# An attention kernel whose hand-written order of work gets a finer model of GpSimd, of the transfer queue and of a ring of buffers

## The chip, the cores and the metric

The kernel runs on one core of one Trainium2 chip. The core has five engines that run in parallel, each in the order of its own instruction list: TensorE (PE, matrix products), VectorE (DVE), ScalarE (ACT), GpSimd (POOL) and SyncE (SP, which only starts transfers). They work on an on-chip memory and on PSUM, the accumulators that PE writes. The metric is the time of one execution in microseconds (us), as the device counts it. The kernel before takes 2528.87 us, median of 3 runs (2528.14 to 2532.28).

## What is computed

Four residual layers on one sequence of S = 2048 rows of D = 512, with H = 32 heads of 16: layers A, B, A, B. A is softmax attention; B is linear attention with a learned feature map. Cut to what matters:

```python
def _A_ref(x, wqkv, wo):
    q, k, v = qkv[0], qkv[1], qkv[2]
    scores = jnp.einsum("bhqd,bhkd->bhqk", q, k) * (Dh ** -0.5)
    p = _softmax(scores, axis=-1)
    o = jnp.einsum("bhqk,bhkd->bhqd", p, v)
    return o.transpose(0, 2, 1, 3).reshape(B, S, D) @ wo
def _B_ref(x, wqkv, w_phi, wo):
    pq, pk = einsum("bhsd,hdf->bhsf", q, w_phi), einsum("bhsd,hdf->bhsf", k, w_phi)
    phi = concatenate([softmax(p), softmax(-p)])          # of q and of k
    o = phi_q (phi_k^T v) / (phi_q (phi_k^T 1) + 1e-6)
    return o.reshape(B, S, D) @ wo
x = x + _A_ref(_layernorm(x), ...); x = x + _B_ref(_layernorm(x), ...)   # twice
```

## The kernel before

Each attention layer has 32 **groups**: a group is a set of four heads (g, eight of them; two make an *octet*) and one block j of 512 queries. A group goes over 16 tiles of 128 keys, in two halves each, so a layer has 1024 **score tiles**. For a score tile PE does eight matmuls (`score_cols`, line L1171 of the profile; 0.217 us in the planner, `UNIT`), and ACT takes the exponential of 128x1024 scores into a buffer p (L1178). For two tiles together PE does a **value step** (`pvs`, L1221; `STEP`, 0.864 us), p against the values v, into an accumulator that lives for the group. Accumulators and all side work share two slots of PSUM, `double` and `pm`; `take()` gives out the one that came free first. About one tile in 40 has its exponential done by DVE instead (`power_task`, twelve instructions L1189 to L1209 on a PSUM slot; the text calls it a **power**).

At a group's end `norm_task` runs: two transposes on DVE empty the accumulator (`turned_sum`, L870), POOL adds the halves (L873), DVE forms the reciprocal (`rec`, L941 and L943) and the product `yn` (L948). Beside this PE has **side streams**: the projections of the next octet (`cols`, L702, in units of 0.217 us), whose results DVE and POOL turn into keys, queries and values (`kq_task`, `values_task`), the output projection of finished octets (`part`, `tail`), and in the first layer the scaling of weights (`prep_b`). Buffers with the tag yt form a ring of four: `turned_sum` and `kq_task` take them in turn, and a buffer of values is in use until SP has written it out in 16 transfers.

Two kinds of task take a **maximum over partitions** on POOL. `norms_task` (L923, nma) does it for each octet's norms, and from it okt and the shift row sh, which the keys of the octet need. `scale_task` (L345) does it for the weights of the next layer (sAo, sB, sBv and sBo, in the first layer). At the end of the program the smallest of all shifts (`lowest`, L1818) decides by such a maximum (`anybad`, L1822, then `flag`, L1824) whether a slower version has to be run. These four instructions are not in the hand-written order; the framework places them on their engines as early as their inputs are.

The order of all this on PE, DVE, ACT and POOL is written out when the kernel is built. `attention` steps a planner's clock `pe`. At each step it takes, in this order, a score tile when a score buffer is free, side work if it ends in time, or a value step if `pe + STEP <= max(due, free) + LATE` (due is when ACT would run dry). Tasks for DVE and POOL are generators which yield an engine, a cost in us and a rank; `Plan.advance` puts them on the two engines' clocks by rank and by when they are ready, and the instructions are emitted in that order. A cost that is too low thus lets an instruction be put ahead of one that would have been ready sooner; on the chip the engine then waits at it. `pairs(g)` starts the transfers that lay out the keys and queries of four heads, and `landed` is the time at which the planner takes them as done.

Of the kernel before, what the change touches and what calls it, by code (L numbers as in the profile page):

```python
# [9 lines left out]
F32 = mybir.dt.float32  # L10
# [7 lines left out]
P = 128  # L18
# [32 lines left out]
FAR = 1e9  # L51
# [6 lines left out]
LEAD = 8  # L58
REST = 0.0
VBUSY = 0.4  # L60
LATE = 0.15
SIDE = 0.0
# [9 lines left out]
def mha_hedgehog_stack(ctx, tc, x_in, a_wqkv, a_wo, b_wqkv, b_wphi, b_wo, out, shmin=SHMIN):  # L72
# [8 lines left out]
    np_ = pool("np", bufs=2)  # L81
# [253 lines left out]
    def scale_task(ms, name):  # L335

        m1 = ms[0]
        for i, m in enumerate(ms[1:]):
            yield "V", 0.17, 3
            t = cp.tile([P, 1], F32, name=f"{name}_m1{i}")  # L340
            nc.vector.tensor_tensor(t, m, m1, ALU.max)
            m1 = t
        yield "P", 1.0, 3
        mm = cp.tile([P, 1], F32, name=name + "_mm")
        nc.gpsimd.partition_all_reduce(mm, m1, P, bass_isa.ReduceOp.max)  # L345
# [448 lines left out]
    class LayerA:  # L794
# [37 lines left out]
        def take(self):  # L832
# [7 lines left out]
            return idx, [pair[:, h, :] for h in range(2)]  # L840

        def freed(self, idx):
            self.pfree[idx] = self.plan.end + 0.15
# [20 lines left out]
        def turned_sum(self, idx, ps, name, rank=0):  # L864

            ys = []
            for u in range(2):
                yield "V", 0.68, rank
                ys.append(np_.tile([P, 16, 32], F32, tag="yb" if u else "yt", name=name + str(u), bufs=2 if u else 4))
# [3 lines left out]
            nc.gpsimd.tensor_tensor(ys[0], ys[0], ys[1], ALU.add)  # L873
            return ys[0]

        def values_task(self, o, j, idx, ps):

            q = self.oct[o]
            yt = yield from self.turned_sum(idx, ps, "vyt")
            for a in range(4):  # L880
                for m in range(4):
                    dst = q["v"][32 * m:32 * m + 32, j * 528:(j + 1) * 528].rearrange("p (t x) -> p t x", x=132)
                    nc.sync.dma_start(dst[:, :, 33 * a + 1:33 * a + 33], yt[32 * a:32 * a + 32, m:16:4, :])  # L883

        def kq_task(self, o, j, ten, idx, ps, sqs):
# [3 lines left out]
            lo = stg[:, 0 if ten else 3, j * 512:(j + 1) * 512]  # L889
            cqk = con["qk"]  # L890
            yield "V", 0.75, 0
            tq = np_.tile([P, 512], F32, tag="yt", name="tq", bufs=4)
            nc.vector.tensor_scalar(tq, ps[0], cqk, None, op0=ALU.mult)
# [8 lines left out]
            yield "V", 0.7  # L902
            nc.vector.tensor_tensor(lo, tq, hi, ALU.subtract)

        def square_task(self, hi, sqs):
# [3 lines left out]
        def norms_task(self, o, i, idx, psn):  # L909
# [10 lines left out]
            nc.vector.tensor_reduce(m, q["nm"], AX.X, ALU.max)  # L920
            yield "P", 5.5
            mm = sp.tile([P, 1], F32, name="nma")
            nc.gpsimd.partition_all_reduce(mm, m, P, bass_isa.ReduceOp.max)  # L923
            yield "P", 1.5
            sh = self.shift_tile()
# [8 lines left out]
        def norm_task(self, G, idx, acc):  # L934

            g, j = self.groups[G]
            o, par = g // 2, g % 2
            yt = yield from self.turned_sum(idx, acc, "yt", -1)
            yield "V", 0.17, 0
# [5 lines left out]
            if par == 0:  # L945
                yn_hold[(o, j)] = np_.tile([P, 16, 32], F32, tag="yn", name="yn", bufs=5)
            yn = yn_hold[(o, j)]
            nc.vector.tensor_tensor(yn[:, :, par * 16:par * 16 + 16], yt[:, :, 1 - par:17 - par],  # L948
                                    rec.unsqueeze(2).to_broadcast([P, 16, 16]), ALU.mult)
            if par == 0:  # L950
                return
# [3 lines left out]
            yb = np_.tile([P, 512], F32, tag="yb", name="yb")  # L955
# [396 lines left out]
        def attention(self, extra, nxt):  # L1352
# [8 lines left out]
            plan = self.plan  # L1361
# [8 lines left out]
            def pairs(g):  # L1370
                self.alloc_pairs(g)
                self.load_pairs(g)
                self.landed[g] = plan.now + 16.0

# [8 lines left out]
            estart, slots, acc, pvdone = [], [0.0] * 6, {}, 0  # L1383
            pe = act = 0.0
            power, pxfree, rested = set(), 0.0, 0.0
            lost = 0.0
            with tc.manual_schedule(engines=COMPUTE):
                while pvq or any(s.gens for s in self.streams):
# [35 lines left out]
                    for turn in range(2):  # L1424
# [14 lines left out]
                        elif ready:  # L1439
                            G, kt = pvq[0]  # L1440
                            if (G in acc or min(self.pfree) <= pe) and pe + STEP <= max(due, free) + LATE:
# [16 lines left out]
                                break  # L1458
                        if turn == 0 and tiles and pxfree <= pe and rested <= pe and plan.clock["V"] <= pe + VBUSY:
                            n = NT * tiles[0][0] + tiles[0][1] + LEAD  # L1460
                            G, kt = n // NT, n % NT
                            if 0 < G < POWERS and self.groups[G][0] in self.kq and plan.now >= self.landed[self.groups[G][0]] and pvq[0][0] in acc and \
                               NT - pvq[0][1] >= 3 and min(self.pfree) <= pe and pe + UNIT <= max(due, free):
                                power.add((G, kt, 1))
                                pxfree, rested = FAR, pe + REST
                                idx, ps = self.take()
# [398 lines left out]
```

## Time and profile before

| | before |
|---|---|
| median of 3 runs | 2528.87 us |
| the profiled execution's own time | 2528.14 us |
| its span | 2526.1 us |
| granted clock of PE, mean | 0.987 |
| attention of layer 1 | 71 to 1027 us |
| layer B after it, with the next layer's start | 1027 to 1338 us |
| attention of layer 3 | 1338 to 2276 us |

A profile page has the busy time of each engine, the span in 40 slices, the chain of work that ended last, and the costliest groups of instructions. A group's row has line, engine, operation, output and inputs, count, then busy time, mean duration in ns, the idle time before these instructions and what ended it. A row of the timeline has start in us, duration in us, engine, line, operation and operands, the count merged into the row, and in brackets the idle time of that engine before it with what ended it ("issue" is idle time in which the engine waited for nothing that the trace shows).

### The profile page before, as it was taken

The numbers are of one execution on the slowest core, as the hardware profiler recorded it, in microseconds if no ns is written. First come the engines' busy times: TensorE is split into PE (matmuls) and PEld (weight loads), VectorE is DVE, ScalarE is ACT, GpSimd is POOL, SyncE is SP. The second block draws the span as 40 slices with busy tenths as digits, with TensorE's granted clock in tenths as the row PEclk, the third lists the DMA queues.
The fourth block names the chain that finished last, engine by engine and source line by source line (L and its number), as shares of the span: only waits on it lengthen the run. The fifth ranks groups of instructions, "written<-read, shape, count | busy, mean of one in ns | idle before, by whom it ended". The sixth has DMA issues, their size and how long they took to land.

```text
span 2526.1 us, 103429 instructions
## 1 busy us (share of the span) xinstructions
PE 2314.9 (92%) x46698; PEld 1090.1 (43%) x46698; DVE 1618.7 (64%) x2883; ACT 2129.0 (84%) x2378; POOL 535.2 (21%) x645
## 2 busy tenths in 40 slices
PE   6999998999999999889789999999899999998998
PEld 4444444444434444445344444444344344444543
DVE  8365636756666455889963666565575652468897
ACT  6999998999999999544438999999999999994553
POOL 3111111111111000366431112112111100005552
PEclk9999999999999999999889999999999999999999
DMA  5310530133036421100133004203300341110003
GB/s 194 66 27 8 87 64 18 53 46 57 3 92 160 140 81 57 35 18 17 68 95 62 17 7 61 34 3 51 64 3 11 72 135 63 60 69 26 9 18 110
DMA packets 114924, 142.85 MB, mean 57 GB/s; under 512 B 64184, under 2 KB 69928, under 8 KB 112168
## 3 DMA queue, kind: packets, MB, share of 16 engines
q1 hardware_dynamic: 113288, 133.38, 21.5%
q8 instruction: 367, 6.01, 1.0%
q0 software_dynamic: 1184, 2.77, 0.3%
q14 instruction: 85, 0.70, 0.1%
HBM read 62.16 MB, written 41.94 MB: 41 GB/s over the span
## 4 chain that ended last, share of the span: by engine, by line
ACT 51%; PE 20%; DVE 13%; issue 12%; POOL 3%; SPq 1%; DMA 1%; ACTq 0%; POOLq 0%; DVEq 0%
ACT p L1178 49%; PE s L1171 4%; PE double L1221 4%; PE pm L1221 2%; DVE su L1591 2%; PE pm L702 2%; PE po L685 1%; PE pbv L1521 1%; PE pk L1521 1%; POOL f L1600 1%; DVE f L1583 1%; SPq L883 1%; DVE f L1584 1%; DVE mx L1580 1%; PE pq L1521 1%
## 5 line engine op out<-in xcount | busy, mean ns | idle before, releaser
L1178 ACT ACTIVATE p<-s 128x1024 f32<-128x1024 f32 x2000 | 1846.5, 1068 | 47.6 <-PE s L1171 46.1
L1171 PE MATMUL s<-kq 49*32 49x512 f16 x15152 | 789.2, 382 | 96.1 <-ACT p L1178 79.7
L1171 PEld LDWEIGHTS <-kq 49*32 49x32 f16 x15872 | 387.7, 89 | 889.8 <-issue 814.4
L1221 PE MATMUL double<-p,v 64*32 64x512 f32 x8984 | 617.1, 592 | 2.4 <-DVE yt L870 1.1
L1221 PE MATMUL pm<-p,v 64*32 64x512 f32 x7016 | 479.6, 589 | 0.3 <-issue 0.3
L873 POOL TENSOR_TENSOR yt<-yt,yt 128x512 f32<-128x512 f32 x64 | 87.4, 1365 | 863.2 <-DVE yt L870 809.3
L1221 PEld LDWEIGHTS double<-p,v 64*32 64x32 f32 x8984 | 175.0, 106 | 32.1 <-PE pm L702 3.8
L1521 PEld LDWEIGHTS <-xnTa 128*128 128x128 f16 x1152 | 110.7, 98 | 155.2 <-DVE f L1584 28.5
L1600 POOL TENSOR_TENSOR f<-f,su 128x1024 f32<-128x1024 f32 x62 | 119.9, 1934 | 129.3 <-DVE su L1594 104.9
L1221 PEld LDWEIGHTS pm<-p,v 64*32 64x32 f32 x7016 | 136.0, 106 | 24.6 <-issue 2.2
L988 POOL TENSOR_TENSOR sq<-stg 128x512 bf16<-128x512 f16 x48 | 57.1, 1189 | 393.3 <-PE s L1171 293.4
L870 DVE STREAM_TRANSPOSE yt<-double 128x512 f32<-128x512 f32 x72 | 47.3, 696 | 131.5 <-PE double L1221 131.5
L1585 ACT ACTIVATE f<-f,c_pB 128x1024 f32<-128x1024 f32 x64 | 72.7, 1149 | 51.1 <-DVE f L1584 51.0
L1521 PE MATMUL pbv<-wbv,xnTa 128*128 128x512 f16 x384 | 91.6, 390 | 23.8 <-DVE f L1584 23.8
L1255 DVE SCALAR_TENSOR_TENSOR xt<-pm,c_oA,xt 128x512 f32<-128x512 f32 x52 | 38.9, 748 | 100.3 <-PE pm L702 87.5
L1255 DVE SCALAR_TENSOR_TENSOR xt<-double,c_oA,xt 128x512 f32<-128x512 f32 x60 | 44.8, 747 | 89.4 <-PE double L702 88.7
L1606 ACT ACTIVATE fk<-f 128x1024 f16<-128x1024 f32 x30 | 31.7, 1058 | 74.8 <-POOL f L1600 74.8
L702 PEld LDWEIGHTS <-wA 64*32 64x32 f16 x4608 | 75.9, 93 | 39.6 <-issue 1.4
L1521 PE MATMUL pq<-wbqk,xnTa 128*128 128x512 f16 x384 | 88.4, 379 | 0.0
L1521 PE MATMUL pk<-wbqk,xnTa 128*128 128x512 f16 x384 | 88.1, 379 | 0.0
L1591 DVE TENSOR_REDUCE su<-f 128x64 f32<-128x1024 f32 x64 | 77.5, 1211 | 9.5 <-ACT f L1585 8.9
L1203 DVE SCALAR_TENSOR_TENSOR px<-pz,px 128x512 f32<-128x512 f32 x96 | 74.0, 771 | 2.7
(320 smaller groups left out, 3087.9 us busy)
## 6 DMA issues: line engine op xcount, KB each, us to landing
kq<-stg SPq DMA_DIRECT2D x168, 128.0 KB
xd<-xt SPq DMA_DIRECT2D x40, 512.0 KB
xt<-xd SPq DMA_DIRECT2D x40, 512.0 KB
v<-vyt SPq DMA_DIRECT2D x384, 16.0 KB
oD<-osp SPq DMA_DIRECT2D x24, 256.0 KB
ob<-oD SPq DMA_DIRECT2D x8, 768.0 KB
xt<-in_A_x_dram SPq DMA_DIRECT2D x8, 512.0 KB
wbqk<-dBqk SPq DMA_DIRECT2D x2, 2048.0 KB
```

Of the source, the lines that this page charges most:

```text
L702: nc.tensor.matmul(ps[h][c, :], w[r, c], x[r], start=(n == 0), stop=(n == of - 1), skip_group_check=True)
L873: nc.gpsimd.tensor_tensor(ys[0], ys[0], ys[1], ALU.add)
L988: nc.gpsimd.tensor_tensor(sq, hi, hi, ALU.mult)
L1171: nc.tensor.matmul(banks2[u][32 * c:32 * c + 32, :], self.side(g, half, 64 * u, 0, kt * P + 32 * c, 32), self.side(g, half, 64 * u, 1, j * ...
L1178: nc.scalar.activation(pt, s, AF.Exp, scale=EXPS)
L1203: nc.vector.scalar_tensor_tensor(y, z, PB, y, op0=ALU.add, op1=ALU.mult)
L1221: nc.tensor.matmul(acc[h][32 * hh:32 * hh + 32, :], self.oct[o]["v"][r, x:x + 32], pt[r, hh % 2, :], start=(kt == 0), stop=(kt == NT - 1), ...
L1255: nc.vector.scalar_tensor_tensor(xt[:, u, :], ps[h], con["oA"], xt[:, u, :], op0=ALU.mult, op1=ALU.add)
L1521: nc.tensor.matmul(dst, xnT[:, a, c, t * P:(t + 1) * P], w(b, c), start=(i == 0 and c == 0), stop=(i == 2 and c == NC4 - 1))
L1585: nc.scalar.activation(f, f, AF.Exp, scale=con["pB"])
L1591: nc.vector.tensor_reduce(su, f[:, r, :], AX.X, ALU.add)
L1600: nc.gpsimd.tensor_tensor(f3, f3, self.part_sums(f3, slice(0, 64), factor), ALU.mult)
```

## The change

Costs in the planner: `scale_task` puts down 7.6 us instead of 1.0 for the maximum on POOL, `norms_task` 7.4 instead of 5.5 and then 2.1 instead of 1.5. The ring: a task that wants a yt buffer is held back in the plan until the planner's time of the fourth last buffer's release has come (`ring`, "until"); `ringed` takes the buffer, and the release times are set at the buffer's last use, for values by the time of the transfer queue, `self.sp`, plus 2.5. The queue: `self.sp` grows by 0.7 for each of the 16 transfers of values (`queued`) and by 17 for a set of `pairs`, whose `landed` is then `self.sp + 2` instead of the present time + 16. Value steps: `LATE` is 0.2 instead of 0.15. Powers: `REST`, which was 0, goes; in the first layer, before step 100, a power is only taken when no side work is due (`EAGER`). No computation is added or taken away, and no "until" becomes a wait of an engine: all of it moves instructions.

```diff
-REST = 0.0
+RING = 4
+EAGER = (100, 0)
-LATE = 0.15
+LATE = 0.2
@@ scale_task
-        yield "P", 1.0, 3
+        yield "P", 7.6, 3
@@ LayerA
+        def ring(self):
+            return "until", lambda: self.yts[-RING] <= self.plan.now
+        def ringed(self, name):
+            self.yts.append(FAR)
+            return len(self.yts) - 1, np_.tile([P, 16, 32], F32, tag="yt", name=name, bufs=RING)
+        def queued(self, n, cost):
+            self.sp = max(self.sp, self.plan.end) + n * cost
+            return self.sp
@@ turned_sum
+            if rank >= 0:
+                yield self.ring()
@@ values_task
-            yt = yield from self.turned_sum(idx, ps, "vyt")
+            slot, yt = yield from self.turned_sum(idx, ps, "vyt")
+            self.yts[slot] = self.queued(16, 0.7) + 2.5
@@ kq_task
+            yield self.ring()
             yield "V", 0.75, 0
-            tq = np_.tile([P, 512], F32, tag="yt", name="tq", bufs=4)
+            slot, tq = self.ringed("tq")
...
+            self.yts[slot] = self.plan.end + 0.1
@@ norms_task
-            yield "P", 5.5
+            yield "P", 7.4
...
-            yield "P", 1.5
+            yield "P", 2.1
@@ norm_task
+            self.yts[slot] = self.plan.end + 0.1
@@ attention, pairs
-                self.landed[g] = plan.now + 16.0
+                self.sp = max(self.sp, plan.now) + 17.0
+                self.landed[g] = self.sp + 2.0
@@ attention
-            power, pxfree, rested = set(), 0.0, 0.0
+            self.yts, self.sp = [0.0] * RING, 15.0
+            power, pxfree = set(), 0.0
...
-                        if turn == 0 and tiles and pxfree <= pe and rested <= pe and plan.clock["V"] <= pe + VBUSY:
+                        if turn == 0 and tiles and pxfree <= pe and (need is None or self.now >= EAGER[self.li]) and plan.clock["V"] <= pe + VBUSY:
```

What this does to the order is seen at three places. In the rows, the name left of the arrow is written and those right of it are read; numbers behind a name tell buffers apart. Line numbers of the changed kernel are higher by 1 to 28.

The first is on PE at the end of group 14 in the first attention. s is a score tile, a row that reads p is a value step, a row that reads xnT a projection. Before, from the last value step of the group on:

```order
L1221 MATMUL double<-p,v_1036 32x512 x8
L1171 LDWEIGHTS kq_0_6724
L1171 MATMUL s<-kq_0_6724 32x512
...
L702 MATMUL pm_11581<-xnT_0_154,wAv 32x512
...
L1171 MATMUL s<-kq_1_6725 32x512
...
L702 MATMUL pm_11582<-xnT_0_154,wAv 32x512
...
L1221 MATMUL double<-p,v_1036 32x512 x8
```

The first value step of the next group stands two score tiles later, in the same slot, behind two and then five units of projection. The same place in PE's order of the changed kernel:

```order
L1247 MATMUL pm_11018<-p,v_1036 32x512
L1197 LDWEIGHTS kq_0_6892
L1197 MATMUL s<-kq_0_6892 32x512
...
L703 MATMUL double<-xnT_1_155,wAv 32x512
...
L1197 MATMUL s<-kq_1_6893 32x512
...
L1197 MATMUL s<-kq_0_6892 32x512
...
L1247 MATMUL pm_11821<-p,v_1036 32x512
```

Now three score tiles lie between, the second and the third with two units of projection between them, and the value step follows the third. Of the 63 places in both layers where one group follows another, 25 have two tiles between and the same slot before, 23 three tiles and the same slot, and 15 change the slot; in the changed order these are 1, 49 and 12, and one has four tiles.

The second is on DVE in the second attention, around the norms' maximum of the last octet (nmx) and the end check that the framework places there. Before:

```order
L914 TENSOR_REDUCE nm<-pm_41862 128x1
L920 TENSOR_REDUCE nmx<-nm 128x1
L870 STREAM_TRANSPOSE yt_41967<-double 128x512
L870 STREAM_TRANSPOSE yt_41990<-double 128x512
L1818 TENSOR_REDUCE lowest<-okt 32x1
L1820 TENSOR_SCALAR bad<-lowest 32x1
L1189 TENSOR_SCALAR px<-double 128x512
L1192 SCALAR_TENSOR_TENSOR pw<-px,double 128x512
L941 TENSOR_SCALAR rec<-yt_41967 128x16
```

The flag stands ten rows below rec there. In the changed order of DVE the same place reads:

```order
L945 TENSOR_REDUCE nmx<-nm 128x1
L1235 SCALAR_TENSOR_TENSOR px<-pw,px 128x512
...
L1846 TENSOR_REDUCE lowest<-okt 32x1
L1848 TENSOR_SCALAR bad<-lowest 32x1
L1852 CAST flag<-anybad 32x1
L891 STREAM_TRANSPOSE yt_41910<-double 128x512
L891 STREAM_TRANSPOSE yt_41923<-double 128x512
L1215 TENSOR_SCALAR px<-double 128x512
L966 TENSOR_SCALAR rec<-yt_41910 128x16
```

The two transposes of the group's accumulator have moved from ahead of the check to behind its flag. The third place is on DVE at the end of the first attention: xnTa is the third block of the normalized rows, transposed, for layer B, and L1580 is layer B's first operation there. Before:

```order
L564 TENSOR_SCALAR xn<-xt,mv,ly 128x512 x2
L587 CAST xnTa_2_22782<-double 128x4x128
L592 TENSOR_TENSOR xnTa_2_22782<-double,xnTa_2_22782 128x4x128
L870 STREAM_TRANSPOSE yt_23649<-pm_23069 128x512
L870 STREAM_TRANSPOSE yt_23651<-pm_23070 128x512
L941 TENSOR_SCALAR rec<-yt_23649 128x16
L943 RECIPROCAL rec<-rec 128x16
L948 TENSOR_TENSOR yn<-yt_23649,rec 128x16x16
L1580 TENSOR_REDUCE mx<-pk 128x32
```

The transposes that empty the last accumulator come last there. In the changed order they come 24 rows ahead of the first row shown here, which stands among layer B's (L1608 to L1622):

```order
L982 STREAM_TRANSPOSE yb<-yn 128x512
L565 TENSOR_SCALAR xn<-xt,mv,ly 128x512
L985 CAST osp<-yb 128x512
L1612 TENSOR_TENSOR f<-mn,pq 128x32x16
L588 CAST xnTa_2_22881<-double 128x4x128
L1619 TENSOR_REDUCE su<-f 128x64
L593 TENSOR_TENSOR xnTa_2_22881<-double,xnTa_2_22881 128x4x128
```

The statistics, xn and the casts of the third block have moved behind the last transposes; a second cast and subtraction follow these.

More of the change, by code (lines that the diff above doesn't have):

```diff
@@ L868, in turned_sum @@
                 yield "V", 0.68, rank
-                ys.append(np_.tile([P, 16, 32], F32, tag="yb" if u else "yt", name=name + str(u), bufs=2 if u else 4))
+                if u == 0:
+                    slot, yt = self.ringed(name + "0")
+                    ys.append(yt)
+                else:
+                    ys.append(np_.tile([P, 16, 32], F32, tag="yb", name=name + "1", bufs=2))
                 nc.vector.transpose(ys[u].rearrange("p a b -> p (a b)"), ps[u])
@@ L873, in turned_sum @@
             nc.gpsimd.tensor_tensor(ys[0], ys[0], ys[1], ALU.add)
-            return ys[0]
+            return slot, ys[0]
         def values_task(self, o, j, idx, ps):
             q = self.oct[o]
-            yt = yield from self.turned_sum(idx, ps, "vyt")
+            slot, yt = yield from self.turned_sum(idx, ps, "vyt")
+            self.yts[slot] = self.queued(16, 0.7) + 2.5
             for a in range(4):
@@ L890, in kq_task @@
             cqk = con["qk"]
+            yield self.ring()
             yield "V", 0.75, 0
-            tq = np_.tile([P, 512], F32, tag="yt", name="tq", bufs=4)
+            slot, tq = self.ringed("tq")
+            tq = tq.rearrange("p a b -> p (a b)")
             nc.vector.tensor_scalar(tq, ps[0], cqk, None, op0=ALU.mult)
@@ L937, in norm_task @@
             o, par = g // 2, g % 2
-            yt = yield from self.turned_sum(idx, acc, "yt", -1)
+            slot, yt = yield from self.turned_sum(idx, acc, "yt", -1)
             yield "V", 0.17, 0
@@ L1464, in attention @@
                                 power.add((G, kt, 1))
-                                pxfree, rested = FAR, pe + REST
+                                pxfree = FAR
                                 idx, ps = self.take()
```

## The prediction

> **What bounds the kernel now.** I read the page first: the busy shares, then the costliest groups, then the chain that ended last.
>
> ```profile
> PE 2314.9 (92%) x46698; PEld 1090.1 (43%) x46698; DVE 1618.7 (64%) x2883; ACT 2129.0 (84%) x2378; POOL 535.2 (21%) x645
> ACT p L1178 49%; PE s L1171 4%; PE double L1221 4%; PE pm L1221 2%; DVE su L1591 2%; PE pm L702 2%; PE po L685 1%; PE pbv L1521 1%; PE pk L1521 1%; POOL f L1600 1%; DVE f L1583 1%; SPq L883 1%; DVE f L1584 1%; DVE mx L1580 1%; PE pq L1521 1%
> L1178 ACT ACTIVATE p<-s 128x1024 f32<-128x1024 f32 x2000 | 1846.5, 1068 | 47.6 <-PE s L1171 46.1
> ```
>
> PE has the most busy time, but the chain runs for 49% of the span through ACT's exponentials, line L1178. They stand in the two attention stages, so I asked for those two stretches alone (the columns are length, then busy time and count of PE, weight loads, DVE, ACT and POOL, granted clock, DMA share, GB/s).
>
> ```profile
> 71.00:1027.00 956.00, 894.73 (x21465) 410.46 (x21465) 557.69 (x1020) 925.11 (x1001) 114.03 (x111) 1.00 0.27 63
> 1338.00:2276.00 938.00, 881.86 (x21374) 400.56 (x21375) 528.48 (x937) 921.32 (x999) 113.98 (x104) 1.00 0.22 47
> ```
>
> There ACT does 1001 and 999 exponentials and is busy 97 and 98% of the time. Undisturbed they start every 0.915 us: in the row at 496.27 us further below, 31 of them take 28.52 us, so (28.52 - 1.07) / 30. At that pitch they need 916 and 914 us; 40 and 24 us are lost, and nearly all of it before an exponential that waits for PE's scores. So the attention stages can gain at most some 64 us, and a gain is one of scores that come in time. The change touches nothing outside the two stages but the order at their ends.
>
> **Part 1, stalls behind GpSimd and the ring: -12 us.** The longest losses in ACT's timeline were followed back through PE, DVE and POOL:
>
> ```profile
> 429.31 0.38 POOL L345 PARTITION_ALL_REDUCE sAo_mm<-sAo_m  x1 [5.85 <-issue]
> 437.12 1.25 POOL L873 TENSOR_TENSOR yt<-yt,yt 128x512 f32<-128x512 f32 x1 [7.43 <-issue]
> 438.40 0.17 DVE L941 TENSOR_SCALAR rec<-yt 128x16 f32<-128x16 f32 x1 [7.01 <-POOL yt L873]
> 439.30 0.55 PE L1171 MATMUL pm<-kq 49*32 49x512 f16 x7 [4.79 <-DVE tq L895]
> 440.38 1.02 ACT L1178 ACTIVATE p<-s 128x1024 f32<-128x1024 f32 x1 [4.84 <-PE s L1171]
> 442.52 23.94 ACT L1178 ACTIVATE p<-s 128x1024 f32<-128x1024 f32 x26 [1.11 <-PE s L1171]
> ...
> 528.84 1.27 POOL L873 TENSOR_TENSOR yt<-yt,yt 128x512 f32<-128x512 f32 x1 [6.91 <-issue]
> 534.58 1.02 ACT L1178 ACTIVATE p<-s 128x1024 f32<-128x1024 f32 x1 [3.27 <-PE s L1171]
> ...
> 852.21 1.25 POOL L873 TENSOR_TENSOR yt<-yt,yt 128x512 f32<-128x512 f32 x1 [7.10 <-issue]
> 855.36 3.02 ACT L1178 ACTIVATE p<-s 128x1024 f32<-128x1024 f32 x3 [1.56 <-PE s L1171]
> ...
> 136.03 0.75 DVE L893 TENSOR_SCALAR tq<-pm,c_qk 128x512 f32<-128x512 f32 x1 [2.55 <-DMA v<-vyt]
> 138.44 2.10 ACT L1178 ACTIVATE p<-s 128x1024 f32<-128x1024 f32 x2 [1.20 <-PE s L1171]
> ```
>
> A maximum over partitions holds POOL 5.85 us before its 0.38 us record and 6.9 to 7.4 us behind it, before the next sum. The planner had put down 1.0 us for that of a scale, so it placed rec, which needs the next sum, on DVE 7 us too soon; the operations behind rec in DVE's order stood, and with them the PSUM slot that PE wanted. The last pair is another cause: tq waits until the transfers of v have left its ring buffer. In the changed order on DVE, twelve operations of a power stand where rec stood behind sAo, and the same holds at the other maxima I followed, so I let these go: 4.84 + 1.11 + 3.27 + 1.56 + 1.20 = 12 us. What is late next there is nothing that I can find: the next sum on POOL now has no waiter. Bounds: 0 (below) and -14, with the small idle times that follow each.
>
> The wait itself is not added by the change: the new "until" for the ring holds back a task in the plan, not an engine. Only a projection's tq queues behind it in its own stream, and its slot of PSUM stays taken meanwhile.
>
> The page "GPSIMD Engine Reference" of the Trainium skill, section 2.1 on instruction dispatch, says that the first call of freshly loaded code pays about 6 us with no visible instruction. The rows agree (5.85 before, 6.9 to 7.4 behind), and by that rule each maximum holds POOL for two such loads, some 13 us, where the change puts down 7.4 or 7.6: a rule that speaks against it, and the reason for the second rival below.
>
> **Part 2, group ends: -21 us.** When the 16 value steps of a group are through, two transposes of DVE must empty the accumulator before the same PSUM slot serves the next group.
>
> ```profile
> 494.06 0.63 PE L702 MATMUL pm<-xnT,wA 64*32 64x512 f16 x16
> 494.86 1.09 PE L1221 MATMUL double<-p,v 64*32 64x512 f32 x16 [0.17 <-PE pm L702]
> 495.71 0.67 PE L1171 MATMUL s<-kq 49*32 49x512 f16 x16
> ...
> 496.27 28.52 ACT L1178 ACTIVATE p<-s 128x1024 f32<-128x1024 f32 x31 [0.64 <-PE s L1171]
> ...
> 2161.91 29.57 ACT L1178 ACTIVATE p<-s 128x1024 f32<-128x1024 f32 x32 [0.64 <-PE s L1171]
> ```
>
> Here the first value step of the next group follows two score tiles behind the last one, into the same slot, after projection matmuls, and the next scores come too late. I laid PE's order beside ACT's starts: 13 such ends in the first attention and 12 in the second, each with some 0.6 of idle ACT, as in the two rows, or up to 0.9; with the 0.15 by which the pitch is shorter than an exponential that is 0.7 to 1.1 each, 22 us in all. Ends with three tiles between cost 0.04, ends that change the slot 0 to 0.2. In the changed order one such end is left, 50 have three or four tiles between: -21 us, bounds -14 (if a third of the loss stays as value steps are put off) and -22.
>
> **Part 3, value steps closer together: +12 us.** With LATE at 0.2 and value steps put off at the ends, PE has to catch up.
>
> ```profile
> 654.15 0.41 PE L1171 MATMUL s<-kq 49*32 49x512 f16 x8 [0.34 <-ACT p L1178]
> 654.36 1.05 PE L1221 MATMUL double<-p,v 64*32 64x512 f32 x16
> 655.23 0.41 PE L1171 MATMUL s<-kq 49*32 49x512 f16 x8
> 656.30 0.41 PE L1171 MATMUL s<-kq 49*32 49x512 f16 x8
> 656.90 0.41 PE L1171 MATMUL s<-kq 49*32 49x512 f16 x8 [0.18 <-ACT p L1178]
> ```
>
> A tile with a value step takes PE 1.08 us (654.15 to 655.23), 0.165 over the pitch of 0.915. A single one is absorbed by the tile before; of two in a row the second shows. The order before has 62 such pairs, which cost 0.079 us each in ACT's starts, 4.9 us; the order after has 127, most of them in the places (right behind a group end) where those of before cost 0.13 to 0.16. 127 x 0.135 = 17, so +12. Bounds: 65 more at 0.079, +5; all at 0.165, +16. Another 52 tiles with three projection units ahead of a value step, at the 0.048 of the 13 there are now: +2.5. The powers fall from 48 to 47, one exponential more: +0.9.
>
> **Part 4, the check's flag in the second attention: +5.4 us.** The end check of the program (lowest, bad, anybad, flag) is moved up into the second attention by its own dependences. Before, POOL's sum, two powers and rec lay between bad and flag. After, flag is next behind bad on DVE, ahead of the two transposes that free the accumulator.
>
> ```profile
> 1946.89 0.41 PE L998 MATMUL pm<-sq,bones 64*32 64x512 bf16 x8
> 1951.48 0.38 POOL L923 PARTITION_ALL_REDUCE nma<-nmx  x1 [5.96 <-issue]
> 1961.45 0.68 POOL L930 TENSOR_SCALAR sh<-sh,neg 1x512 f16<-1x512 f16 x1
> 1968.19 0.38 POOL L1822 PARTITION_ALL_REDUCE anybad<-bad  x1 [6.06 <-issue]
> ...
> 1976.06 2.10 ACT L1178 ACTIVATE p<-s 128x1024 f32<-128x1024 f32 x2 [1.18 <-PE s L1171]
> ```
>
> From the norms' matmul to the end of nma 5.0 us; 7.0 until POOL's next operation (row at 528.84); 1.1 for okt, neg and sh; 6.06 + 0.38 + 0.1 to the flag; 1.3 for the transposes: 20.9. PE wants the slot for a power 17 tiles behind the norms, 15.6 us. It stalls 5.3 us.
>
> ```profile
> 434.00:439.00 5.00, 0.51 (x17) 0.03 (x2) 0.59 (x2) 1.54 (x2) 1.25 (x1) 1.00 0.02 5
> 439.00:441.00 2.00, 1.70 (x31) 0.92 (x38) 2.00 (x5) 0.62 (x1) 1.09 (x1) 0.61 0.00 0
> 441.00:443.00 2.00, 2.00 (x40) 0.99 (x32) 2.00 (x5) 0.89 (x2) 0.00 (x0) 0.54 0.00 0
> ```
>
> After the 4.79 us stall of PE the granted clock (the third column from the end) is 0.61 and 0.54 and ACT idles 1.11 more; I add 1.2 for that and take off the 1.18 lost there today: +5.4. Bounds: +3 (flag's wait begins earlier than I think) and +9. "TensorE: Matmul & The Clock Gate" of the Trainium skill, Part 1, puts the halving behind an idle window of about 3.4 us; the row agrees, and by that rule a stall of under 3.4 us here would cost nothing more, which makes +4.2.
>
> **Part 5, end of the first attention: +5 us.** The changed order puts transposed casts of the third block (xnTa) and its small statistics behind the last value step, among layer B's first operations.
>
> ```profile
> 1025.39 0.69 DVE L592 TENSOR_TENSOR xnTa<-double,xnTa 128x512 f16<-128x512 f32 x1
> 1029.80 0.45 DVE L941 TENSOR_SCALAR rec<-yt 128x16 f32<-128x16 f32 x1 [1.45 <-POOL yt L873]
> 1037.00:1050.00 13.00, 12.84 (x85) 6.55 (x84) 12.81 (x20) 6.25 (x8) 7.84 (x6) 1.00 0.00 1
> ```
>
> Today these end at 1026, under ACT's last exponentials. After, three pairs of a cast and a subtraction of 0.69 each, nine small ones of about 0.16 and two xn of 0.5 stand behind: 6.7, less the 1.45 in which DVE waited for POOL. The stage behind is full on DVE (12.81 of 13), so it comes through: +5, bounds +2 and +6. The second attention's end is unchanged.
>
> **The sum**, against the profiled execution of 2528.1 us (its span 2526.1 and 2.0 around it; the median of the runs is 2528.9, 0.03% above): -12 - 21 + 12 + 2.5 + 0.9 + 5.4 + 5 = -7.2, so **2521**.
>
> **Rivals.** *Catch-up dearer than the ends.* If pairs come so thick that the slack is not refilled between them, both steps of a pair show, 2 x 0.165 = 0.33; with half of them so, 0.25 each, 127 x 0.25 = 32, minus 4.9 is 27 instead of 12: 2536. From 0.24 a pair the change is slower than before by over 0.2%. For it: the largest single pairs of the trace cost 0.46 to 0.48. Against: none of the ordinary ones costs over 0.17. *POOL's load comes back.* The planned 7.4 or 7.6 holds one load and not two; if the four places of part 1 only move, their 12 us come back: 2533. Against: the sums behind have few waiters. *Flag and tail are hidden*, as their waits end before PE or layer B asks: without 5.4 and 5 it is 2511. *The ends do not gain*, since putting off the value step merely moves the same loss to the next tile (part 2 at -7): 2535; for it speaks only that PE is busy 94% of the stage.
>
> **Chances.** Forecast 0.50 (own range 2514 to 2528), flag and tail hidden 0.20, catch-up dearer 0.12, load comes back 0.13, ends do not gain 0.05. What a measurement of this kernel tells from no change is about 0.2%, 5 us: faster is under 2523.8, slower over 2533.9. Of the forecast 0.38 lies in faster, 0.12 in same; hidden is faster; of the load 0.03 faster, 0.08 same, 0.02 slower; of the dear pairs 0.02 same and 0.10 slower; of the ends 0.02 and 0.03. Faster 0.61, same 0.24, slower 0.15. The range leaves out 0.1 on either side: 2508 to 2534.
>
> **What would show it.** Right: no idle of over 3 us before an exponential of the first attention; ACT idle of 0.6 to 0.9 once per layer instead of 12 times; many idles of 0.1 to 0.2; one PE stall of about 5 us in the second attention with flag on DVE behind it, clock halved after it; xnTa casts beyond the last exponential. Wrong: a stall of PE behind any other maximum, or group ends that still idle ACT by 0.6.

## The result, and the profile after

The changed kernel takes 2510.65 us (median of 6 runs, 2508.70 to 2513.97) against 2529.31 us of the kernel before in the same runs. The ratio is 0.9928, with a 95% interval of 0.9915 to 0.9940: 18 us, or 0.7%, faster. The profiled execution took 2509.21 us, its span is 2507.3. The forecast was 2521 us, its range 2508 to 2534.

The first view is again the page: the chain that ended last, and the group of the exponentials (now line L1204; scores are L1197, value steps L1247).

```profile
ACT p L1204 56%; PE double L1247 2%; PE s L1197 2%; DVE su L1619 2%; PE pbv L1549 1%; PE po L686 1%; PE pk L1549 1%; PE pq L1549 1%; DVE f L1611 1%; PE pm L703 1%; POOL f L1628 1%; DVE f L1612 1%; DVE mx L1608 1%; DVE st L492 1%; DVE su L1620 1%
L1204 ACT ACTIVATE p<-s 128x1024 f32<-128x1024 f32 x2001 | 1852.0, 1064 | 21.7 <-PE s L1197 19.1
```

The chain runs through the exponentials for 56% of the span instead of 49%, and the idle time that waits for PE's scores is 19.1 us instead of 46.1. ACT is bound by the same work as before, with fewer gaps. The windows of the two attention stages (length, then busy time and count of PE, weight loads, DVE, ACT and POOL) say the same by stage:

```profile
71.00:1008.00 937.00, 886.25 (x21422) 407.05 (x21414) 513.58 (x949) 929.04 (x1004) 113.04 (x111) 1.00 0.27 63
1324.00:2256.00 932.00, 874.86 (x21334) 399.09 (x21327) 541.35 (x964) 920.62 (x997) 110.86 (x104) 0.99 0.22 47
```

From the first start of an exponential of a stage to the last, in ACT's timeline, the profiled executions divide like this. "Late" is what the order of DVE has behind the last transposes of that attention of the output sums, statistics, xn and casts of its blocks, in number times duration; 1.9 us of it, the first statistics of the last block, stand there in every order. The time of each exponential beyond the pitch of 0.914 us, added up by size, stands below (exponentials that start sooner than the pitch are left out).

| us | before | changed |
|---|---|---|
| first attention (exponentials) | 953.9 (1001) | 937.0 (1004) |
| layer B and the next layer's start | 313.8 | 315.8 |
| second attention | 935.8 (999) | 932.2 (997) |
| last layer B | 251.6 | 251.7 |
| late at the first, at the second end | 1.9, 1.9 | 8.5, 3.3 |
| losses of 0.6 and more (places) | 44.6 (39) | 14.5 (10) |
| losses of 0.2 to 0.6 | 7.0 | 5.7 |
| losses under 0.2 | 17.3 | 29.0 |

Three views answer to the parts of the prediction. The first is POOL's timeline around the maximum of sAo, and ACT's over the same stretch, with two group ends in it.

```profile
409.61 0.50 POOL L346 PARTITION_ALL_REDUCE sAo_mm<-sAo_m  x1 [5.81 <-DVE sAo_m L342]
424.46 1.18 POOL L1014 TENSOR_TENSOR sq<-stg 128x512 bf16<-128x512 f16 x1 [14.36 <-DVE stg L922]
...
404.01 66.69 ACT L1204 ACTIVATE p<-s 128x1024 f32<-128x1024 f32 x72
```

POOL still stands idle for 5.81 us ahead of the maximum. But its next work waits for DVE anyway and comes 14 us later, so nobody waits for it, and 72 exponentials run without a gap over a stretch in which the kernel before lost 4.84 and 1.11 us to this stall and 0.65 at a group end. The second view is PE's timeline behind a group end:

```profile
477.16 0.41 PE L1197 MATMUL s<-kq 49*32 49x512 f16 x8
477.38 1.06 PE L1247 MATMUL double<-p,v 64*32 64x512 f32 x16
478.24 0.41 PE L1197 MATMUL s<-kq 49*32 49x512 f16 x8
478.46 0.61 PE L1247 MATMUL double<-p,v 64*32 64x512 f32 x4
...
479.32 0.41 PE L1197 MATMUL s<-kq 49*32 49x512 f16 x8
```

Two value steps stand in two tiles in a row; the scores come 1.08 us apart twice, and ACT loses 0.166 at the second. This is the catch-up: 127 such pairs, 21.7 us in ACT's starts, 0.171 each (before 62 pairs and 4.9 us). The third view is the check's flag in the second attention, on DVE, on PE and on ACT, with the clock of PE (third column from the end of the windows):

```profile
1927.52 0.14 DVE L1848 TENSOR_SCALAR bad<-lowest 32x1 f32<-32x1 f32 x1
1934.81 0.14 DVE L1852 CAST flag<-anybad 32x1 int32<-32x1 f32 x1 [7.16 <-POOL anybad L1850]
1934.88 1.29 DVE L891 STREAM_TRANSPOSE yt<-double 128x512 f32<-128x512 f32 x2
1943.30 0.17 DVE L966 TENSOR_SCALAR rec<-yt 128x16 f32<-128x16 f32 x1 [5.68 <-POOL yt L894]
...
1936.23 0.63 PE L1197 MATMUL double<-kq 49*32 49x512 f16 x8 [4.89 <-DVE yt L891]
...
1937.41 1.02 ACT L1204 ACTIVATE p<-s 128x1024 f32<-128x1024 f32 x1 [4.86 <-PE s L1197]
1939.54 15.69 ACT L1204 ACTIVATE p<-s 128x1024 f32<-128x1024 f32 x17 [1.11 <-PE s L1197]
1956.58 9.27 ACT L1204 ACTIVATE p<-s 128x1024 f32<-128x1024 f32 x10 [1.35 <-PE s L1197]
...
1936.00:1938.00 2.00, 1.77 (x32) 0.69 (x39) 0.87 (x2) 0.59 (x1) 0.00 (x0) 0.50 0.00 0
1938.00:1940.00 2.00, 2.00 (x40) 0.70 (x32) 0.00 (x0) 0.89 (x2) 0.00 (x0) 0.50 0.00 0
```

DVE waits 7.16 us for the check's maximum with the two transposes behind it, PE 4.89 us for the accumulator they empty. The clock is at 0.50 for the 4 us that follow, which costs 1.11 more. After that rec waits 5.68 us for POOL's next sum, and a power behind rec in DVE's order comes 1.35 us late.

### The profile page after: what moved, and what is told of

It is laid out like the page before. It is cut to its first block, busy times and chain, and to the rows that moved or that the text cites. A ratio compares the mean times of both kernels' runs of the same rounds, so it can differ in the third digit from the quotient of the medians.

```text
span 2507.3 us, 103429 instructions
## 1 busy us (share of the span) xinstructions
PE 2305.4 (92%) x46698; PEld 1086.9 (43%) x46698; DVE 1596.5 (64%) x2867; ACT 2134.8 (85%) x2379; POOL 531.2 (21%) x645
## 4 chain that ended last, share of the span: by engine, by line
ACT 58%; PE 14%; issue 13%; DVE 12%; POOL 2%; DMA 0%; POOLq 0%; ACTq 0%; DVEq 0%
ACT p L1204 56%; PE double L1247 2%; PE s L1197 2%; DVE su L1619 2%; PE pbv L1549 1%; PE po L686 1%; PE pk L1549 1%; PE pq L1549 1%; DVE f L1611 1%; PE pm L703 1%; POOL f L1628 1%; DVE f L1612 1%; DVE mx L1608 1%; DVE st L492 1%; DVE su L1620 1%
## 5 line engine op out<-in xcount | busy, mean ns | idle before, releaser
L1204 ACT ACTIVATE p<-s 128x1024 f32<-128x1024 f32 x2001 | 1852.0, 1064 | 21.7 <-PE s L1197 19.1
L1197 PE MATMUL s<-kq 49*32 49x512 f16 x15136 | 789.3, 381 | 99.1 <-ACT p L1204 86.1
L1197 PEld LDWEIGHTS <-kq 49*32 49x32 f16 x15872 | 386.0, 89 | 880.6 <-issue 798.5
L1247 PE MATMUL double<-p,v 64*32 64x512 f32 x9064 | 612.8, 591 | 0.0
L1247 PE MATMUL pm<-p,v 64*32 64x512 f32 x6944 | 476.6, 590 | 0.0
L1247 PEld LDWEIGHTS double<-p,v 64*32 64x32 f32 x9064 | 174.0, 106 | 30.9 <-issue 6.4
L1281 DVE SCALAR_TENSOR_TENSOR xt<-pm,c_oA,xt 128x512 f32<-128x512 f32 x102 | 76.2, 747 | 155.0 <-PE pm L703 151.1
L1247 PEld LDWEIGHTS pm<-p,v 64*32 64x32 f32 x6944 | 135.2, 106 | 22.2 <-issue 3.3
L891 DVE STREAM_TRANSPOSE yt<-pm 128x512 f32<-128x512 f32 x56 | 36.8, 696 | 89.9 <-PE pm L1247 89.6
L917 DVE TENSOR_SCALAR tq<-double,c_qk 128x512 f32<-128x512 f32 x28 | 21.0, 749 | 107.0 <-PE double L703 103.7
```

The source lines that it names most:

```text
L1197: nc.tensor.matmul(banks2[u][32 * c:32 * c + 32, :], self.side(g, half, 64 * u, 0, kt * P + 32 * c, 32), self.side(g, half, 64 * u, 1, j * ...
L1204: nc.scalar.activation(pt, s, AF.Exp, scale=EXPS)
L1247: nc.tensor.matmul(acc[h][32 * hh:32 * hh + 32, :], self.oct[o]["v"][r, x:x + 32], pt[r, hh % 2, :], start=(kt == 0), stop=(kt == NT - 1), ...
L1281: nc.vector.scalar_tensor_tensor(xt[:, u, :], ps[h], con["oA"], xt[:, u, :], op0=ALU.mult, op1=ALU.add)
```

## The experiments

Theory A: the new costs of the maxima keep work that depends on POOL away from them, and that removes the stalls. Theory B: LATE alone moves the group ends, and the stalls go because the ends no longer meet the maxima. The first four kernels tell them apart; from their results came theory C, on the ends of the attentions.

**LATE alone, and all but LATE.** The edit of the first is to the kernel before, that of the second to the changed one:

```diff
-LATE = 0.15
+LATE = 0.2
```

> The kernel before with LATE 0.2 and nothing else. Its order has no group end left with two tiles between in the same slot (25 before), 132 pairs of value steps in consecutive tiles (62 before), four exponentials fewer, and the flag right behind bad on DVE as in the changed kernel. Both theories: group ends -22.2, pairs (at 0.171 us each, the mean in the changed kernel's trace) +17.7, exponentials -3.7, flag +5: together -3.2 us. Theory A, the new costs on POOL remove the stalls behind the maxima: the 12 us of stalls stay, so about 2526 us. Theory B, the stalls go because LATE moves the group ends away from the maxima, whatever the costs say: about 2514 us.

```diff
-LATE = 0.2
+LATE = 0.15
```

> The changed kernel with LATE back at 0.15: only costs, transfer queue, ring and EAGER. 23 group ends with two tiles between in the same slot, 57 pairs, five exponentials more than before (+4.6 us), the flag right behind bad (+5). Theory A (costs remove the stalls): -12 us on top, about 2526 us. Theory B (LATE moves the group ends): the stalls stay or change places, about 2537 us.

LATE alone: 2538.21 us, ratio 1.0032 (1.0020 to 1.0044), slower than before; its profiled execution, 2544.54 us, is one of the slowest of the nine. The rest alone: 2525.36 us, ratio 0.9982 (0.9973 to 0.9991). The sum of the two is +0.1%; together they make -0.7%. The edits don't add, since each lays the whole order anew. For the second kernel theory A's number came out (2526), and its only loss over 3 us in the first attention, at 342 us, is PE's wait of 3.24 us for a transfer of layer B's weights, with no maximum near. For the first kernel neither number did. Its group ends are gone as expected, but its trace has new stalls. Two come behind maxima: 2.6 us at 542, where PE waits for the transfers of the shift row, which come out of a norms' maximum, and 2.4 at 860. There DVE stands in front of sBv's maximum, the output sums (xt) stand behind it on DVE, and PE and ACT wait for them:

```profile
855.67 0.15 DVE L347 TENSOR_SCALAR sBv_mm<-sBv_mm 128x1 f32<-128x1 f32 x1 [6.59 <-POOL sBv_mm L345]
857.63 0.37 PE L702 MATMUL pm<-woA,ob 64*32 64x512 f16 x1 [1.14 <-DVE xt L1255]
859.91 3.02 ACT L1178 ACTIVATE p<-s 128x1024 f32<-128x1024 f32 x3 [2.21 <-PE s L1171]
```

The largest loss of the first attention, 4.1 us at 806, where PE waits for output sums too, has no maximum near. And the stage between the attentions takes 329.3 us instead of 313.8, which neither theory had.

**The old costs of the maxima in the changed kernel.**

```diff
-        yield "P", 7.6, 3
+        yield "P", 1.0, 3
...
-            yield "P", 7.4
+            yield "P", 5.5
...
-            yield "P", 2.1
+            yield "P", 1.5
```

> The changed kernel with the old costs of the maxima on POOL (1.0, 5.5 and 1.5). The same group ends and pairs as in the changed kernel. Theory A: the stalls of 12 us come back, about 2522 us. Theory B: nothing but the stall behind sBv, whose next sum stands again right behind the maximum (1.6 us in the trace before): 2510.5 to 2513 us.

2521.72 us, ratio 0.9967 (0.9954 to 0.9980); the profiled execution was the fastest, 2515.18. The stalls come back, at another maximum: sB at 772.84 us, with POOL's, DVE's, PE's and ACT's rows.

```profile
780.04 1.26 POOL L894 TENSOR_TENSOR yt<-yt,yt 128x512 f32<-128x512 f32 x1 [6.82 <-issue]
781.34 0.17 DVE L966 TENSOR_SCALAR rec<-yt 128x16 f32<-128x16 f32 x1 [5.59 <-POOL yt L894]
782.89 0.37 PE L703 MATMUL pm<-woA,ob 64*32 64x512 f16 x1 [1.86 <-DVE pw L1218]
785.02 0.41 PE L703 MATMUL pm<-woA,ob 64*32 64x512 f16 x7 [1.75 <-DVE pw L1218]
785.76 1.02 ACT L1204 ACTIVATE p<-s 128x1024 f32<-128x1024 f32 x1 [3.53 <-PE s L1197]
...
806.17 1.02 ACT L1204 ACTIVATE p<-s 128x1024 f32<-128x1024 f32 x1 [4.81 <-PE s L1197]
```

This is the mechanism of sAo in the kernel before, row for row: the sum 6.82 us behind the maximum, rec ahead of a power's first operations, PE's slot. So B falls, and the mechanism of theory A holds, here and at 860 us in LATE alone. Its number came out in part by luck. The 4.81 us at 806 come 20 us later and follow output sums (xt) that stand between the operations of a power on DVE; kernels below that keep the new costs lose 2.4 to 5.1 us at about this place too. And the stage between the attentions takes 311.0 us instead of 315.8. How much of the gain the new costs bring by themselves is not shown.

**The check as a planned task.** In the changed kernel the four instructions of the check become a task behind the last norms' maximum, so that the planner sets them in order:

```diff
+            if self.li == 1 and o == 3:
+                self.spawn(self.check_task(), self.plan.end - self.plan.now + 0.15)
+        def check_task(self):
+            yield "V", 0.17
...
+            yield "P", CHK
...
+            nc.gpsimd.partition_all_reduce(anybad, bad, 32, bass_isa.ReduceOp.max)
+            yield "V", 0.17
```

> The changed kernel with the end check put into the hand-written order as a task behind the last norms' maximum, with 14 us for its maximum on POOL: its flag then stands behind other work on DVE, and the transposes ahead of it. Theory: the idle times of ACT at 1931.5 (5.0 less the pitch), 1937.4 (1.22) and 1954.1 (1.52) go, 6.4 to 7.7 us, about 2503.5 us. Rival: the maximum holds POOL for two loads anyway, and the rec of the next group end takes over the stall: 2509 to 2511 us.

2519.12 us, ratio 0.9960 (0.9948 to 0.9973): slower than the changed kernel by 8 us, where both theories had it as fast or faster. The stall itself went as expected: the second attention takes 922.7 us instead of 932.2. But the last layer B takes 267.4 instead of 251.7. Its start, in the windows, first of the changed kernel and then of this one:

```profile
2256.00:2276.00 20.00, 18.25 (x113) 8.13 (x112) 18.69 (x33) 6.00 (x8) 8.47 (x7) 1.00 0.05 19
...
2250.00:2270.00 20.00, 12.25 (x92) 5.14 (x76) 18.88 (x42) 4.50 (x5) 4.36 (x3) 0.85 0.16 53
```

DVE is as busy as before, PE a third less. What DVE does there is late work of block 2, and its rows, PE's and POOL's show the price:

```profile
2250.86 0.75 DVE L1300 SCALAR_TENSOR_TENSOR xt<-pm,c_oA,xt 128x512 f32<-128x512 f32 x1 [1.56 <-PE pm L704]
2251.85 1.31 DVE L892 STREAM_TRANSPOSE yt<-double 128x512 f32<-128x512 f32 x2 [0.24 <-PE double L1266]
...
2270.60 2.62 DVE L566 TENSOR_SCALAR xn<-xt,mv,ly 128x512 f32<-128x512 f32 x2
...
2271.20 1.11 PE L1336 MATMUL pm<-ident,xn 128*128 128x128 f32 x4 [5.94 <-DVE xn L566]
...
2286.93 1.93 POOL L1647 TENSOR_TENSOR f<-f,su 128x1024 f32<-128x1024 f32 x1 [11.42 <-DVE su L1641]
```

The last output sum of block 2 comes one row ahead of the last accumulator's transposes. So its statistics and xn, one after the other, are strewn among layer B's first operations until 2273 us, PE waits for xn with layer B's products behind, and POOL waits 11 us. This made theory C: an attention's end costs by how much of block 2's chain stands behind the last transposes on DVE.

**Theory C tested by four orders.** The first differs from the last kernel by one number:

```diff
-CHK = 14.0
+CHK = 11.0
```

> As the run with the planned check, but its maximum on POOL is put down with 11 us instead of 14. Checked by order: the flag stands at the same distance behind bad, but block 2's last projections, statistics and casts end ahead of the second attention's last transposes but for 3.3 us of DVE's rows (10.8 us with 14; 3.3 in the changed kernel). Theory C, the loss of the run before is this late work at the attention's end: layer B behind the second attention takes 252 us again instead of 267 and the attention stays at 923 to 924, so about 2501 us. Rival: planning the check costs layer B something of its own (its flag is read there): 2515 to 2520 us.

2505.99 us, ratio 0.9909 (0.9892 to 0.9925). The last layer B takes 251.7 us, the attention 927.8, and ACT runs through where the flag's stall was: 45 exponentials in one row, while the flag is set 4 us behind its maximum's record.

```profile
1924.21 41.62 ACT L1223 ACTIVATE p<-s 128x1024 f32<-128x1024 f32 x45
...
1942.61 0.38 POOL L972 PARTITION_ALL_REDUCE anybad<-bad  x1 [5.86 <-DVE px L1248]
1947.23 0.14 DVE L975 CAST flag<-anybad 32x1 int32<-32x1 f32 x1
```

Theory C holds, and its rival falls. The sum missed by 5 us: the attention was 4 us over what was expected, and the stage between the attentions 1.5.

The second takes the model of the transfer queue out for `pairs`, in the changed kernel:

```diff
-                self.sp = max(self.sp, plan.now) + 17.0
-                self.landed[g] = self.sp + 2.0
+                self.landed[g] = plan.now + 16.0
```

> The changed kernel with keys and queries of four heads taken as landed 16 us after the present time, as before, so without the model of the transfer queue for them. The late rows of DVE are 4.7 us at the first attention's end (8.5 in the changed kernel) and 10.8 at the second's (3.3). Theory C: the last layer B takes some 267 us, the first stage between the attentions 311 to 314, two exponentials fewer, so 2510.7 + 15.5 - 3 - 1.8 = about 2521 us. If the queue model itself removes waits of PE for transfers of kq (2.6 and 4.1 us of idle ACT in the run of LATE alone), these come on top: about 2527 us, with PE rows ended by DMA kq in the trace.

2541.79 us, ratio 1.0055 (1.0039 to 1.0072). That is 15 us over the higher of the two numbers expected. The last layer B takes 267.0 us, the stage between 311.5, both as theory C has them. The rest is waits for transfers, as the other theory had them, but larger and at another engine: DVE, then PE, then ACT.

```profile
571.30 0.43 DVE L922 TENSOR_SCALAR stg<-tq 128x512 f16<-128x512 f32 x1 [9.04 <-DMA kq<-sh]
576.33 1.05 PE L703 MATMUL double<-xnT,wA 64*32 64x512 f16 x16 [8.78 <-DVE pw L1218]
577.94 1.03 ACT L1204 ACTIVATE p<-s 128x1024 f32<-128x1024 f32 x1 [9.18 <-PE s L1197]
```

The one buffer stg, from which the transfers of kq read, is written anew by the next octet's keys; DVE stands 9.04 us in front of it. (The profile names the transfers of the shift row, which follow in the queue; the last transfer out of stg was issued at 566.32 us.) With the queue in the plan DVE waits there too (twice, 8.8 us in all, in the changed kernel), but the first attention has no loss over 1.4 us, so nothing that ACT needs is behind it.

The third allows powers ahead of step 100 in the first attention again:

```diff
-EAGER = (100, 0)
+EAGER = (0, 0)
```

> The changed kernel with powers allowed ahead of step 100 in the first attention even when side work is due, as before. Seven exponentials fewer (-6.4 us) and seven powers more; late rows of DVE 10.8 us at the first attention's end (8.5 in the changed kernel), 3.3 at the second's. Theory C: 10.8 rows cost some 13 us more between the attentions, so 2510.7 - 6.4 + 13 = about 2517 us. Rival: the early powers only fill idle time on DVE and the end is hidden: about 2504 us. A second rival: they hold up the projections of the first octet, waits of several us before 150 us: 2520 to 2530 us.

2523.42 us, ratio 0.9974 (0.9963 to 0.9986). No wait came up ahead of 150 us, so the second rival falls, though the time lies in its range. The stage between the attentions takes 322.2 us, 6.4 more than in the changed kernel (13 expected). The first attention takes 4.5 us more: it has seven exponentials fewer and loses that time again to stalls (5.12 us at 801, 2.68 at 886). The second takes 3.6 us more with the same order, so that part is not of the edit. What is gained by EAGER is thus which order came out, not the time ahead of step 100.

The fourth puts both loads of a maximum into the plan, in the kernel with the short check:

```diff
-        yield "P", 7.6, 3
+        yield "P", 13.0, 3
...
-            yield "P", 7.4
+            yield "P", 13.0
```

> The kernel with the short planned check, with 13.0 us put down for each maximum on POOL (both loads) instead of 7.4 and 7.6. If the changed kernel's cost, which holds one load, leaves waits behind the maxima, these go: the idle of ACT in the attentions falls by a few us. Theory C: late rows of DVE are 13.3 us at the first attention's end and 10.8 at the second's, so the stage between the attentions takes some 329 us and the last layer B 267, together 28 us more than with the short planned check: about 2529 us. Rival: the late rows are hidden and it is 2500 us or less.

2529.49 us, ratio 1.0001 (0.9992 to 1.0011). The ends cost in the direction of theory C, 324.4 and 263.5 us: 19 us more than with the short check, where 28 were expected. The attentions don't gain in sum: 942.3 and 926.5 against 937.6 and 927.8; a loss of 4.44 us at 575, again with DVE's stg behind the transfers of kq, is new. That the sum came out at 2529 us is luck. So in this order the one load in the plan left nothing to gain. "GPSIMD Engine Reference" of the Trainium skill, section 2.1, has about 6 us for the load of fresh code; the rows agree (5.81 ahead of sAo, 6.82 behind sB), but in this order the place of a maximum decided, not its full price in the plan.

**No powers in the last two groups that had them, and the changed kernel again.** In the kernel with the short check:

```diff
-POWERS = 26
+POWERS = 24
```

> The kernel with the short planned check, with no powers in the groups 24 and 25 of each attention (POWERS 24). Four exponentials more (+3.7 us); the late rows of DVE at the two attention ends fall from 8.5 and 3.3 us to 1.9 and 1.9. Theory C: the stage between the attentions falls from 317 to 311 to 314 us, where the other runs with 1.9 stand, and the last layer B stays at 252: about 2506 us, no gain in the sum. Rival: the late rows of the first attention's end are hidden behind PE's first projections of layer B, and the exponentials alone count: about 2510 us.

> The changed kernel, unaltered, on the same chip as the run beside it: 2508 to 2513 us as before; the first and the second attention at 937 and 932 us within 3 us, for the stages of other runs whose order is the same differ by that much.

With fewer powers 2510.83 us, ratio 0.9917 (0.9903 to 0.9930). That is the rival's number, but not its reason: the stage between falls to 311.6 as theory C has it, but the first attention takes 942.8 us, with two stalls around 800 us. The changed kernel on the same chip: 2512.76 us, ratio 0.9931 (0.9917 to 0.9944), its stages 938.5, 317.4, 932.7 and 253.3 us. The version with the short check has the lowest ratio of all; its interval overlaps with the changed kernel's, so it is not shown to be faster.

Stage by stage, over all twelve executions (late work of the end ahead of the stage):

| late work, us | stage between the attentions, us | last layer B, us |
|---|---|---|
| 1.9 | 313.8, 311.0, 311.6 | 251.6, 253.0, 253.6 |
| 3.3 | | 251.7, 253.2, 251.7, 251.7, 251.5, 253.3 |
| 4.7 | 311.5 | |
| 8.0 to 8.5 | 316.7, 315.8, 318.4, 317.3, 317.4 | |
| 10.8 | 322.2 | 267.4, 267.0, 263.5 |
| 13.3 | 329.3, 324.4 | |

The spread of this table has a measure in it. Three executions have the same order on DVE, POOL and ACT behind the first attention, with 1.9 us of late work: 313.8 (the kernel before), 311.0 and 311.6, in the mean 312.1. Four others share the changed kernel's order there: 315.8, 317.4, 318.4 and 317.3, in the mean 317.2. So the changed order costs 5.1 us there, and single executions of one order lie up to 2.8 us apart.

**The ring.** With the ring's "until" always true, the changed kernel comes out as the same program, instruction for instruction. The ring never holds a task back here; it is no part of the result.

## Why the prediction was right, and where its sizes were off

The direction and the range held; of the likeliest case's own range, 2514 to 2528, the time lies 3 us below. The terms, against the spans (2526.1 to 2507.3, -18.8; forecast -7.2):

- **Stalls and group ends, forecast -12 and -21.** The losses of 0.6 us and more, without those at the flag, fall from 43.3 to 6.8 us: -36.5. Right, with the small losses behind each stall on top, which the forecast left to its bounds. That the costs of the maxima have to do with it was shown by putting them back; that LATE takes away the group ends was shown by LATE alone, which has none left, and by the rest alone, which keeps 23.
- **Pairs, forecast +12, at most +16.** 127 pairs at 0.171 make +16.7, over the bound: I took 0.135 from the places of before, and behind a group end nearly every pair pays the full 0.165. But the step that went with it, three projection units ahead of a value step (+2.5), costs nothing (65 places, 0.3 us in all), and the other intervals, among them those with prep_b's work, lose some 6 us less. All losses under 0.6 together rise by 10.4 us where 14.5 were forecast.
- **One exponential more, +0.9.** 2001 instead of 2000.
- **The flag, +5.4.** 5.0, 1.2 and 1.5 in the place of 1.3: +6.4. The chain from the norms to the flag, PE's stall of 5.3 us (4.89 measured) and the clock behind it came as worked out; the late power (1.5) was not foreseen. The rule of "TensorE: Matmul & The Clock Gate" of the Trainium skill, Part 1, of half the clock behind an idle window of about 3.4 us agrees with the 0.50 of the windows. What the prediction concluded from it, that a stall of under 3.4 us would cost nothing more, does not hold: behind PE's stall of 3.24 us at 340 us in the kernel with the rest alone the clock is 0.65 and then 0.50 over 4 us, and ACT idles 1.11 us more.
- **The end of the first attention, forecast +5, bounds +2 and +6.** +2.0 in this pair of executions, at the lower bound. Over all executions of the two orders it is +5.1, so the price was right: the kernel before lies at the upper end of its spread here and the changed one at the lower end of its own. What makes that spread stays open. The prediction called the second attention's end unchanged; there one cast and one subtraction have moved behind the last transposes (late work 3.3 instead of 1.9), but the last layer B takes 251.7 us after 251.6.
- **The rest** of some 2 us is that exponentials behind a late one start at less than the pitch (1.6), and the start (0.3).

The difference of 11.6 us is thus 3.5 in stalls and group ends, 4.1 in the small losses, 3.0 at the first attention's end, which is spread between executions, and some 2 in the rest, less 1.0 at the flag. The step that was sized worst is part 3: a pair costs more than I took, and what stands around the pairs less. Of the rivals, dearer catch-up fell (0.171, not 0.24). The load of POOL coming back fell for this order: no loss of the first attention is over 1.4 us, and putting both loads into the plan gained nothing. Flag and tail were not hidden. That this rival's number, 2511, is the measured one is a coincidence: the time came from the other terms. Group ends without gain fell.

One thing the prediction did not say is how much of the result belongs to this very order. It read the changed order as it stood, and that carried it. A forecast edit by edit would have failed: LATE alone is slower, and taking away the queue or EAGER costs 1.3 and 0.5%, by stalls and attention ends that neither edit names.

## What to carry to other kernels

Where a planner lays out the order, a changed cost moves everything behind it: read the new order at the waits of the old trace, and then at the places that were quiet, the ends of a stage above all. A value step or product that is put off at a boundary is paid back in pairs, whose price is the excess of one interval over the bound engine's pitch, nearly in full each time. Work that the framework places outside the plan, such as the flag here, belongs into the plan, and its effect has to be measured with the stage that follows.

## What was not expected of the hardware

The second attention took 932.2, 932.7 and 935.8 us in three executions with the same order of score tiles and value steps on PE; what makes such a difference was not followed. The transfers out of stg held DVE for 9.04 us, more than any of its waits for POOL behind a maximum, the longest of which was 8.4 us. And a stall of 4.9 us on PE cost the next 4 us at half the clock again, 1.1 us of ACT's time, as behind the stall of 4.8 us in the kernel before and one of 3.24 us in the kernel with the rest alone.
